# One more transfer from GpSimd, 40 single words from each partition, between attention and routing

## The chip, the cores and the metric

The kernel runs on one core of a Trainium2 chip. The metric is the device time of one execution in microseconds (us); of several executions the median is given. The core has five engines that run at the same time, each with its own instruction queue: TensorE (PE, with its weight loads as PEld), VectorE (DVE), ScalarE (ACT), GpSimd (POOL) and SyncE (SP). The 16 DMA engines move data between DRAM and the on-chip memory (SBUF). An engine or a queue waits for another only where a semaphore says so.

## What is computed

Two stages, in float32. The first is attention with a block mask: 4 batches, 8 heads, 768 positions, 64 wide, blocks of 32. A query block sees its neighbours, the first and last block, and three blocks drawn for it. The second stage routes the 3072 rows that come out to 8 experts of 384 rows each, greedily by the largest logit, and applies the expert's two matrices:

```python
logits = x @ w_gate                      # x: 3072 x 512, 8 experts
order = np.argsort(-logits.flatten())
for idx in order:                        # largest logit first
    tok, e = int(idx) // E, int(idx) % E
    if assigned[tok] >= 0 or counts[e] >= cap:   # cap = 384
        continue
    assigned[tok] = e; counts[e] += 1
...
h = np.maximum(x[mask] @ w1[e], 0.0)     # for each expert's rows
out[mask] = h @ w2[e]
```

## The kernel before

`tile_kernel` runs `Attn(...).run(start)` and then `Moe(...).run(start)`. Both write out one fixed order of instructions for each engine; the hardware keeps that order within an engine, and semaphores order the engines among each other.

Attention works on pairs of heads and groups of four query blocks. A planner (`Plan`) chooses the order. The rows that it produces go to the DRAM tile `xrows` by SyncE's queue (L628, L638, L640), the logits stay in SBUF as `lg`. GpSimd copies keys and values into place (L276, L370), clears a part of a tile (the memset of L423) and issues gathers of value rows (L401). In the second of the four batches GpSimd also fills the constants of `Start.consts`, among them `places` (L1353): 128 partitions, each holding the numbers 0 to 383 as float32. It is read by `Moe.rows` later and stays in place to the end.

Routing (`Moe.route`, `Moe.search`) finds the expert that fills first and its threshold, by counting how many logits lie above a guess: VectorE counts two thresholds (`jd`) and ScalarE one (`ja`), TensorE sums over the partitions (`pz`), VectorE makes the next guess (`jn`). Two such searches of eight steps stand ahead of the choice of the first expert. Before them `Start.part(1, ...)` prepares the last third of the keys on VectorE (L1383 to L1402). Once the expert is known (`en`, `ei`), GpSimd adds a large negative number to that expert's logits (`lg<-lg,en`), and VectorE takes the next maximum (`c_mx<-lg`). SyncE then loads the first pieces of that expert's weights (`raw`, L1116).

`Moe.rows` turns the threshold into the list of 384 rows, using `places` (`L`) and a running count (`c_M`), and GpSimd gathers those rows from `xrows` in three gathers of 128 (`xg<-xrows,row`). TensorE transposes them and the expert's products begin. From there on the routing of the next experts runs beside the products of the present one. GpSimd then makes the low halves of the weights (`wlo<-raw,whi`), issues the next gathers, and scatters the results (`out_dram<-ot,idx`). Calls in `Moe` that go through the helper `Timed` all bear its line, L816.

All transfers that GpSimd issues are on the queue q0 (software_dynamic), those of SyncE on q1, those of ScalarE on q10.

Of the kernel before, what the change touches and what calls it, by code (L numbers as in the profile page):

```python
# [7 lines left out]
F32 = mybir.dt.float32  # L8
# [1396 lines left out]
def tile_kernel(tc, q, k, v, sampled_blocks, moe_w_gate, moe_w1, moe_w2, out):  # L1405
    nc = tc.nc
    with ExitStack() as ctx:
        ctx.enter_context(tc.manual_schedule())
        cst = ctx.enter_context(tc.tile_pool(name="cst", bufs=1))
        dram = ctx.enter_context(tc.tile_pool(name="dram", bufs=1, space=bass.MemoryType.DRAM))  # L1410
        xd = dram.tile([NT, DM], F32, name="xrows")
        lg = cst.tile([128, NCH, E], F32, name="lg")
        jp = cst.tile([128, 128], I32, name="jp")
        nc.gpsimd.iota(jp, pattern=[[1, 128]], base=0, channel_multiplier=-1)
        ident = cst.tile([128, 128], F32, name="ident")
        nc.vector.tensor_scalar(ident, jp, 0.0, None, op0=OP.is_equal)
        start = Start(nc, cst, lg, jp, ident)
        with ExitStack() as a:
            vs = [dram.tile([S + BS, VR], F32, name=f"vrows{b}") for b in range(B)]
            Attn(a, tc, q, k, v, sampled_blocks, moe_w_gate, xd, vs, lg, ident).run(start)  # L1420
        with ExitStack() as m:
            Moe(m, tc, xd, lg, start.c, moe_w1, moe_w2, out).run(start)


# [27 lines left out]
```

## Time and profile before

| | |
|---|---|
| median of 3 runs | 658.86 us (656.57 to 661.0) |
| profiled execution | 663.22 us, of which the profile's span is 661.4 us |
| mean granted TensorE clock | 0.935 |
| busy, share of the span: TensorE | 563.3 us, 85% |
| VectorE | 423.8 us, 64% |
| GpSimd | 407.2 us, 62% |
| ScalarE | 379.9 us, 57% |
| DRAM traffic | 76.38 MB read, 19.24 MB written |

A share of the span is a mean over stages that differ. What one instruction more is worth is read from the stage in which it stands: attention up to about 302 us, the choice of the first expert up to about 340 us, and the experts from then on. Times in the rows below are us from the start of the span, lengths are us or, where marked, ns.

### The profile page before, as it was taken

The numbers are of one execution on the slowest core, as the hardware profiler recorded it, in microseconds if no ns is written. First come the engines' busy times: TensorE is split into PE (matmuls) and PEld (weight loads), VectorE is DVE, ScalarE is ACT, GpSimd is POOL, SyncE is SP. The second block draws the span as 40 slices with busy tenths as digits, with TensorE's granted clock in tenths as the row PEclk, the third lists the DMA queues.
The fourth block names the chain that finished last, engine by engine and source line by source line (L and its number), as shares of the span: only waits on it lengthen the run. The fifth ranks groups of instructions, "written<-read, shape, count | busy, mean of one in ns | idle before, by whom it ended". The sixth has DMA issues, their size and how long they took to land. (4 is left out here: it accounts for less than half of the span.)

```text
span 661.4 us, 20156 instructions
## 1 busy us (share of the span) xinstructions
PE 563.3 (85%) x7416; PEld 445.7 (67%) x7416; DVE 423.8 (64%) x1630; ACT 379.9 (57%) x846; POOL 407.2 (62%) x741
## 2 busy tenths in 40 slices
PE   5798888789979988863149999999999999999993
PEld 3476656577737765651038788787878878898982
DVE  3677768568756878825776868778786968232110
ACT  4866697558755786624346475565757555445510
POOL 5686757568746876530036485676757677878631
PEclk9898899799989999966568999999999999999997
DMA  9998889887889563300053542626354545445100
GB/s 191 259 229 199 234 223 231 177 225 200 190 183 264 139 172 112 100 18 25 1 164 139 191 161 86 217 82 213 106 192 151 168 144 176 169 166 169 71 16 32
DMA packets 125571, 102.25 MB, mean 155 GB/s; under 512 B 81185, under 2 KB 99745, under 8 KB 125473
## 3 DMA queue, kind: packets, MB, share of 16 engines
q1 hardware_dynamic: 117696, 78.44, 44.0%
q0 software_dynamic: 6912, 22.17, 11.2%
q8 instruction: 58, 0.95, 0.6%
q10 hardware_dynamic: 864, 0.36, 0.2%
q14 instruction: 41, 0.33, 0.2%
HBM read 76.38 MB, written 19.24 MB: 145 GB/s over the span
## 5 line engine op out<-in xcount | busy, mean ns | idle before, releaser
L816 POOL TENSOR_TENSOR wlo<-raw,whi 128x512 fp32r<-128x512 f32 x128 | 161.8, 1291 | 60.6 <-ACT whi L816 60.0
L272 ACT ACTIVATE vw<-vn 32x520 f32<-32x520 f32 (+2 forms) x108 | 68.6, 635 | 29.1 <-PE ps L577 26.7
L276 POOL COPY vw<-vn 32x520 f32<-32x520 f32 (+2 forms) x88 | 54.1, 615 | 46.6 <-DMA vz<-vrows,vidx 22.9
L370 POOL COPY kg<-kT 128x128 f32 x264 | 63.9, 294 | 30.0 <-issue 24.2
L816 PE MATMUL po<-whi,hh 128*128 128x512 f32 x192 | 77.4, 403 | 0.0
L816 PE MATMUL po<-whi,hl 128*128 128x512 f32 x192 | 77.0, 401 | 0.0
L816 PE MATMUL po<-wlo,hh 128*128 128x512 f32 x192 | 76.4, 398 | 0.0
L816 ACT ACTIVATE whi<-raw 128x512 fp32r<-128x512 f32 x128 | 74.2, 621 | 0.2 <-issue 0.2
L482 PE MATMUL ps<-kg,qT 64*32 64x256 f32 x1408 | 57.0, 397 | 14.7 <-POOL kg L370 11.9
L524 DVE TENSOR_REDUCE mn<-ps 128x2 f32<-128x512 f32 x88 | 56.5, 681 | 12.1 <-PE ps L482 11.9
L529 DVE TENSOR_TENSOR s<-ps,mn 128x512 f32<-128x512 f32 x88 | 57.7, 680 | 6.7 <-PE ps L550 6.3
L816 DVE SCALAR_TENSOR_TENSOR hl<-ph,hh 128x384 fp32r<-128x384 f32 x64 | 35.3, 552 | 39.8 <-ACT hh L816 39.8
L816 PE MATMUL ph<-xhi,whi 128*128 128x384 f32 x256 | 59.3, 349 | 0.4 <-ACT xhi L816 0.3
L556 ACT ACTIVATE aT<-ps 128x512 f32<-128x512 f32 x88 | 49.5, 598 | 17.2 <-PE ps L550 10.6
L816 PE MATMUL ph<-xhi,wlo 128*128 128x384 f32 x256 | 58.6, 347 | 0.0
L816 PE MATMUL ph<-xlo,whi 128*128 128x384 f32 x256 | 57.7, 342 | 0.0
L816 ACT ACTIVATE hh<-ph 128x384 fp32r<-128x384 f32 x64 | 31.2, 488 | 45.6 <-PE ph L816 43.8
L550 PE MATMUL ps<-ident,s 128*128 128x128 f32 x352 | 51.4, 287 | 3.5 <-ACT aT L556 1.7
L577 PE MATMUL ps<-vz,aT 128*32 128x65 f32 x1408 | 47.4, 225 | 6.4 <-issue 6.3
L401 POOL DMA_INDIRECT vz<-vrows,vidx x48 | 44.8, 934 | 12.8 <-issue 5.8
L577 PE MATMUL ps<-vw,aT 128*32 128x65 f32 x1408 | 46.6, 227 | 6.0 <-issue 4.9
L482 PEld LDWEIGHTS ps<-kg,qT 64*32 64x32 f32 x1408 | 26.9, 109 | 33.0 <-POOL kg L370 17.3
(226 smaller groups left out, 1246.5 us busy)
## 6 DMA issues: line engine op xcount, KB each, us to landing
raw<-in_moe_w_dram SPq DMA_DIRECT2D x64, 512.0 KB
vz<-vrows SPq DMA_DIRECT2D x120, 65.0 KB
vrows<-vn SPq DMA_DIRECT2D x12, 520.0 KB
st<-in_k_dram SPq DMA_DIRECT2D x24, 256.0 KB
st<-in_q_dram SPq DMA_DIRECT2D x24, 256.0 KB
vn<-in_v_dram SPq DMA_DIRECT2D x24, 256.0 KB
xrows<-xt SPq DMA_DIRECT2D x20, 256.0 KB
vz<-vn SPq DMA_DIRECT2D x12, 260.0 KB
```

The lines of the kernel that those rows point to most:

```text
L272: nc.scalar.activation(o, i, AF.Copy, scale=scale)
L276: nc.gpsimd.tensor_copy(o, i)
L370: nc.gpsimd.tensor_copy(kg()[:, :, g, 128 + 32 * r:160 + 32 * r], kT()[:, :, bass.ds(pv[3 * g + r] * BS, BS)])
L401: nc.gpsimd.indirect_dma_start(out=vz[0:96, g], out_offset=None, in_=self.vs[b], in_offset=bass.IndirectOffsetOnAxis(ap=self.vidx[:, bl[g] ...
L482: nc.tensor.matmul(x["S"][0][32 * g:32 * g + 32, 256 * j:256 * j + 256], qT[h, p, BS * bl[gi]:BS * bl[gi] + BS], kg[h, p, gi], start=True, ...
L524: nc.vector.tensor_reduce(x["mn"][:, 0:2], x["S"][0].rearrange("p (j y) -> p j y", j=2), axis=AX.X, op=OP.min)
L529: nc.vector.tensor_tensor(x["s"].rearrange("p (j t) y -> p j (t y)", j=2), x["S"][0].rearrange("p (j y) -> p j y", j=2), x["mn"][:, 0:2, N ...
L550: nc.tensor.transpose(ps[:, c - c0], x["s"][:, c], self.ident)
L556: nc.scalar.activation(x["aT"][:, c0:c1], x["ps", c0][:, 0:c1 - c0], AF.Exp, scale=-1.0 if w == 4 else 1.0)
L577: nc.tensor.matmul(av[32 * g:32 * g + 32, 2 * j + s], aT[:, 2 * j + t, 32 * g:32 * g + 32], v[:, gi, h], start=t == 0, stop=t == 1)
L816: return f(*args, **kw)
```

## The change

After attention's last instruction and before routing's first, in program order, a DRAM tile of 128 x 40 x 2 words is made, and GpSimd issues a transfer of the first 40 words of each partition of `places` to it. The words lie one behind the other in SBUF; in DRAM every second word is written. 5120 words of 4 bytes are moved, 20 KB. Nothing reads the DRAM tile.

```diff
@@ -1419,6 +1419,8 @@
             vs = [dram.tile([S + BS, VR], F32, name=f"vrows{b}") for b in range(B)]
             Attn(a, tc, q, k, v, sampled_blocks, moe_w_gate, xd, vs, lg, ident).run(start)
         with ExitStack() as m:
+            fill = dram.tile([128, 40, 2], F32, name="fill")
+            nc.gpsimd.dma_start(fill[:, :, 0], start.c["places"][:, 0:40])
             Moe(m, tc, xd, lg, start.c, moe_w1, moe_w2, out).run(start)
```

## Rows read from the trace of the kernel before

**Rows 1.** The page's 40 slices of the span, busy tenths.

```profile
POOL 5686757568746876530036485676757677878631
...
DMA  9998889887889563300053542626354545445100
```

**Rows 2.** Stretches: us, busy us and instructions by engine, clock, DMA share, GB/s.

```profile
core 0: us, PE busy (x) PEld busy (x) DVE busy (x) ACT busy (x) POOL busy (x), PEclk, DMA share, GB/s
...
305.00:310.00 5.00, 0.70 (x5) 0.41 (x5) 3.88 (x24) 1.90 (x7) 0.00 (x0) 0.50 0.00 0
...
315.00:320.00 5.00, 0.66 (x4) 0.32 (x4) 3.81 (x25) 1.65 (x6) 0.00 (x0) 0.50 0.01 3
...
325.00:330.00 5.00, 0.97 (x4) 0.74 (x5) 3.46 (x20) 1.10 (x4) 0.08 (x1) 0.50 0.00 0
```

**Rows 3.** GpSimd's timeline, 280 to 345: start, us, what [idle before <-releaser].

```profile
292.31 0.53 POOL L423 MEMSET vw<- 32x520 f32 x1
329.92 0.59 POOL L816 TENSOR_TENSOR lg<-lg,en 128x192 f32<-128x192 f32 x1 [37.09 <-DVE en L816]
340.30 1.01 POOL L816 DMA_INDIRECT xg<-xrows,row  x1 [9.78 <-DVE pk L816]
...
342.87 0.95 POOL L816 DMA_INDIRECT xg<-xrows,row  x1 [0.30 <-issue]
```

**Rows 4.** Waits of GpSimd, 290 to 345: us in total, times, longest.

```profile
POOL lg L816 <- DVE en L816: 37.1, 1, 37.1
```

**Rows 5.** VectorE's timeline, 329 to 333.

```profile
331.33 0.15 DVE L816 TENSOR_SCALAR ei<-ef 128x1 int32<-128x1 f32 x1
331.40 0.34 DVE L816 TENSOR_REDUCE c_mx<-lg 128x24 f32<-128x192 f32 x1
```

**Rows 6.** GpSimd's groups by form: busy us, mean ns, idle before.

```profile
L401 POOL DMA_INDIRECT vz<-vrows,vidx x48 | 44.8, 934 | 12.8 <-issue 5.8 <-POOL vw L276 1.5 <-DMA vz<-vrows 1.2
...
L816 POOL DMA_INDIRECT out_dram<-ot,idx x24 | 23.7, 989 | 35.0 <-ACT ot L816 32.6 <-issue 1.3 <-ACT ja L816 0.6
L816 POOL DMA_INDIRECT xg<-xrows,row x24 | 23.1, 964 | 16.1 <-DVE pk L816 10.3 <-issue 4.6 <-PE po L816 0.3
```

**Rows 7.** The page's DMA queues: packets, MB, share of 16 engines' span.

```profile
q1 hardware_dynamic: 117696, 78.44, 44.0%
q0 software_dynamic: 6912, 22.17, 11.2%
...
q10 hardware_dynamic: 864, 0.36, 0.2%
```

**Rows 8.** TensorE's timeline, 343 to 350: the transposes of the gathered rows.

```profile
343.80 0.52 PE L816 MATMUL po<-ident,xg 128*128 128x128 f32 x3 [0.28 <-DMA xg<-xrows,row]
...
348.11 0.55 PE L816 MATMUL po<-ident,xg 128*128 128x128 f32 x3 [2.11 <-DMA xg<-xrows,row]
```

**Rows 9.** Scans into c_M (ns min/median/max), and VectorE and GpSimd around the longest.

```profile
L816 DVE TENSOR_TENSOR_SCAN c_M<-c_one,ac x7: 206/209/1285, 333.5 to 557.1; 128x24 bf16<-128x24 f32 x7
...
557.14 1.26 DVE L816 TENSOR_TENSOR_SCAN c_M<-c_one,ac 128x24 bf16<-128x24 f32 x1
...
555.79 2.55 POOL L816 TENSOR_TENSOR wlo<-raw,whi 128x512 fp32r<-128x512 f32 x2 [0.74 <-ACT whi L816]
```

**Rows 10.** VectorE's timeline, 302 to 307: instructions with two inputs in SBUF.

```profile
304.88 0.22 DVE L1390 TENSOR_TENSOR c_eq<-lg,c_mx 128x64 bf16<-128x64 f32 x1
...
305.25 0.22 DVE L1397 TENSOR_TENSOR c_KLi<-c_KLi,c_KHi 128x64 int32<-128x64 int32 x1
```

**Rows 11.** Beside a gather: GpSimd and VectorE near 533, and VectorE's group by form.

```profile
533.13 0.95 POOL L816 DMA_INDIRECT xg<-xrows,row  x1 [0.30 <-issue]
...
533.44 0.14 DVE L816 TENSOR_SCALAR ki<-c_W 128x1 int32<-128x1 f32 x1
...
L816 DVE TENSOR_SCALAR ki<-c_W 128x1 int32<-128x1 f32 x7 | 1.0, 145 | 0.0
```

**Rows 12.** SyncE's queue, 290 to 346: attention's last stores.

```profile
299.69 1.19 SPq L638 DMA_DIRECT2D xrows<-xm  x2
```

## Prediction before the run

> **What bounds the kernel now.** Start with the page's row of 40 slices for GpSimd and for DMA: in the 19th and 20th slice, 45% to 50% of the span, both are at 0 [rows 1]. This is the stretch between attention and the experts, where the first expert is being chosen. The table of stretches says what runs there: VectorE is busy 3.5 to 3.9 of every 5 us, TensorE under 1, GpSimd 0.00 to 0.08, and the DMA share is 0.01 at most [rows 2]. So the end is set here by one serial chain: a threshold search that goes from VectorE to TensorE and back. Nothing on it waits for GpSimd or for a transfer until the choice is made. TensorE's granted clock is 0.50 there, its 1.2 GHz level, because it has only a few small products to do; the change gives it none and takes none.
>
> The timeline of GpSimd then tells exactly when its work is next wanted. Its last attention instruction is the memset at 292.31, which ends at 292.84. The next one is the add on lg at 329.92, after that come three gathers from 340.30 on [rows 3]. The view of waits puts the 37.1 us before the add down to VectorE's en [rows 4]: GpSimd is early, not late. And the add itself has a little room: it ends at 330.51, while the VectorE reduction that reads its result starts at 331.40, right behind ei [rows 5]. GpSimd can thus be 0.89 us late without cost. The room for the new instruction is 331.40 - 0.59 - 292.84 = 37.97 us.
>
> From the gathers on the room is gone: TensorE waits 0.28 and 2.11 us for gathered rows to land [rows 8]; each us by which they come later moves expert 0 and all that follows by about a us.
>
> **The change, part by part.** Nothing is removed or moved. Added are one DRAM tile and one transfer issued by GpSimd. Its source was written by GpSimd itself long before (the iota on places belongs to constants placed during attention), and nobody reads the destination. So the transfer waits for no engine, and no instruction waits for its data. It can cost in three ways only: the time GpSimd spends issuing it, the time the DMA engines spend on it ahead of something that is wanted, and what it takes from VectorE meanwhile.
>
> *Issuing.* The trace of before holds no plain transfer issued by GpSimd, so its price is bounded. The nearest rows are the gathers: 934 ns with 96 rows, 964 ns with 128 [rows 6]. The growth is 30 ns for 32 rows, 0.94 ns a row. The destination keeps every second word, so there are 128 x 40 = 5120 separate pieces. By growth: 0.964 + (5120 - 128) x 0.00094 = 5.7 us. From below: a single instruction that doesn't grow, 0.93 us. From above: the whole 964 ns spread over 128 rows, 7.53 ns a piece, so 38.6 us. I take 5.7 us, because a plain strided piece has no index to be read, and because the only growth shown is the small one; both gathers differ a little in row length, so the slope is rough and I keep the ends. With 0.30 us to issue (the gap ahead of the third gather [rows 3]) it starts near 293.1 and ends near 298.8; by the ends at 294.1 or 331.7. The reader of lg needs GpSimd free by 330.81 (331.40 less the add's 0.59). Cost: 0, 0 and 0.9 us. What hides it is the search on VectorE; without that cover it would cost its whole length, since the add and the gathers are queued right behind it on GpSimd.
>
> *The DMA engines.* The 5120 pieces over 16 engines are 320 for each, taken as evenly shared. The page's queues give a time per packet: q10, the smallest packets (mean 417 B), 0.2% of 16 x 661.4 us over 864 packets, 24 ns; q1 (mean 666 B) 44.0% over 117696, 39.6 ns; q0 (mean 3.2 KB) 11.2% over 6912, 171 ns [rows 7]. For 320 pieces: 7.8, 12.7 or 54.9 us. I take 12.7 us, the middle: these words are nearer to small packets, but q10's share of 0.2% is rounded to one digit, and q1's packets are many and go both ways. From 294 the transfer is then over before 312. Between 305 and 330 the DMA share is 0.01 or less [rows 2], so it is in nobody's way; ahead of that only attention's last stores run, issued up to 300.9 [rows 12], and what they store is first read by the gathers at 340. Cost 0; by the farthest row see rival A.
>
> *VectorE.* Its instructions of the search run beside the gathers later at their usual length. Cost 0; the other end is rival B.
>
> *Tail.* The program's end has one more transfer to be sure of, done 330 us earlier: 0.
>
> **Sum.** 0 + 0 + 0 + 0. Against its own execution: span 661.4 us, run 663.22 us, so 663.2 us after; the bounds of issuing alone make it 663.2 to 664.1. That execution lies 0.7% above the median of the three runs shown, 658.86 us, and a change of nothing leaves the median too: 659.0 us.
>
> **The rivals.** A, *the words drain slowly (slower)*. The gathers go through the same queue q0, the only one of the software kind, so they stand behind the words. It decides from 340.30 + 1.01 - 294.1 = 47 us of drain, 147 ns a word. At q0's 171 ns the drain ends at 349, 7.7 us past the moment when the first gather starts moving, and TensorE's waits for the gathers [rows 8] pass it on whole: 658.9 + 7.7 = 666.6 us. Beyond that each 3.1 ns more a word is 1 us. For it: no row shows single words written to DRAM. Against it: q0's price belongs to packets 800 times larger. The Trainium skill (DMA: Bandwidth & Descriptors, "Queues, rings and completion order") has every engine take one queue's descriptors in order and turn between queues; by that rule the gathers wait behind the words and the weight loads on q1 don't.
>
> B, *VectorE is held while GpSimd issues (slower)*. VectorE's scan into c_M, with two inputs in SBUF, took 1.26 us where its median is 0.209: it ends just behind GpSimd's pair of subtractions (555.79 + 2.55) [rows 9]. The search's preparation has two such instructions, at 304.88 and 305.25 [rows 10]. If the new transfer held VectorE as the subtraction does, they would wait for its end. That decides from 304.88 - 293.1 = 11.8 us of issuing; at 38.6 us the price is 331.7 - 304.88 = 26.8 us, 685.7 us in all; at the 5.7 us that I take it is nothing. Against it: a single-input instruction from SBUF at 533.44, with a gather in progress from 533.13, took 0.14 us, its mean [rows 11]; no view I read has a two-input one beside a gather. The Trainium skill (SBUF — State Buffer, "SBUF: two separate sides") speaks of an exclusive lock on the pair of ports that VectorE and GpSimd share, held for a whole instruction, also against VectorE instructions with two inputs in SBUF if GpSimd's instruction reads SBUF. By the rule, if it counts the transfer, the end is this rival's; by the row at 533.44 it is the sum above.
>
> C, *the words don't go one by one*. In before 48 x 96 + 48 x 128 = 10752 gathered and scattered rows [rows 6] (scatters counted with 128) went in 6912 packets of q0 [rows 7]: fewer packets than rows, so several pieces can share one. Then the drain is shorter still, and the time the same 659 us.
>
> D, *issuing costs more than the gathers' mean*. From 8.6 ns a piece the chain is over 1% late (8.6 x 5120 ns and 0.30 us to issue are 44.3 us, 6.4 us more than the 37.97 of room); at 10 ns it is 51.5 us, 13.5 us late: 672 us. No row speaks for it but the lack of a row.
>
> **How the numbers follow.** Hidden as summed 0.63; C 0.10, same time; A 0.12; B 0.07; D 0.04; and 0.04 for a median that lands lower by the runs' own spread, since no step gains anything. About 1% is what a measurement of this kernel can tell from no change. Within 1%: 0.63 + 0.10 = 0.73; slower by more: 0.12 + 0.07 + 0.04 = 0.23; faster: 0.04. The range starts just under the lowest run before (656.57) and reaches over A's 666.6 to 668; it holds C, the sum and about two thirds of A, some 0.81, and leaves out B, D and a slower drain. The sum's own range is 655.5 to 663.
>
> **What would show it.** GpSimd's timeline: a transfer right behind 292.84, near 6 us long; the idle time before the add on lg down from 37.1 to about 31; the add and the reduction behind it at their old distance from en. If the add starts later than 0.9 us after en, issuing was mis-sized (D). If VectorE's instruction at 304.88 is long or late, B. If the DMA share stays up past 340 and the gathers' landing grows beyond the 2.11 us wait, A. What would make the forecast wrong, above all, is that no row of before writes single words to DRAM: both bounds of the drain come from longer packets.

## The result, and the profile after

The time after is 666.1 us (median of 16 runs, 662.07 to 670.97); beside it on the same chip the kernel before took 662.36 us (16 runs, 656.57 to 665.78). The ratio is 1.0076, with a 95% interval from 1.0052 to 1.0099 (the two medians alone give 1.0056): slower by three quarters of a per cent. (The forecast's 659.0 us rests on the three runs of before shown then; over sixteen before stands at 662.36.) That lies within the 1% of the forecast and within its range, but it is not "no change", and the reasons given for no change do not hold. Two effects of opposite sign lie under it, and the prediction had neither; that they leave so small a sum is luck.

The profiled execution took 664.25 us, its span 662.5. GpSimd first, which is where the prediction looked (start, us, what, idle before):

```profile
290.79 0.53 POOL L423 MEMSET vw<- 32x520 f32 x1
291.27 2.01 POOL L1423 DMA_DIRECT2D fill<-c_places  x1
336.00 0.58 POOL L816 TENSOR_TENSOR lg<-lg,en 128x192 f32<-128x192 f32 x1 [42.72 <-DVE en L816]
346.36 1.03 POOL L816 DMA_INDIRECT xg<-xrows,row  x1 [9.78 <-DVE pk L816]
```

Issuing took 2.01 us and was over at 293.3. GpSimd then waited 42.72 us for VectorE's en, longer than the 37.09 of [rows 3], so GpSimd is even earlier than before. The add on lg and the first gather are 10.4 us apart in both kernels (336.00 to 346.36; 329.92 to 340.30). What came late is VectorE, and it was late already at the first reduction of routing, here in after and then in before:

```profile
310.33 0.21 DVE L1383 TENSOR_REDUCE c_mx<-lg 128x8 f32<-128x64 f32 x1 [11.44 <-issue]
```

```profile
304.27 0.21 DVE L1383 TENSOR_REDUCE c_mx<-lg 128x8 f32<-128x64 f32 x1 [4.61 <-issue]
```

It starts 13.7 us after attention's last value products (L577) end at 296.6; in before it starts at 304.27, 5.6 us after theirs at 298.7. From this reduction to the add the distance is 25.7 us in both. So the search itself, the stretch that the prediction studied, lost nothing; 8.1 us went just ahead of it. ScalarE shows where, in after and, for the copy to lp, in before:

```profile
295.72 0.59 ACT L272 ACTIVATE xT<-ps 128x512 f32<-128x512 f32 x1
303.93 0.28 ACT L272 ACTIVATE lp<-ps 128x128 f32<-128x128 f32 x1 [7.62 <-remote]
304.89 0.18 ACT L272 ACTIVATE lg<-ps 128x8 f32<-128x8 f32 x1 [0.69 <-PE ps L680]
```

```profile
298.97 0.28 ACT L272 ACTIVATE lp<-ps 128x128 f32<-128x128 f32 x1 [0.59 <-PE ps L669]
```

The copy to lp waits for TensorE's product of L669. In before the same copy started at 298.97 after 0.59 us of waiting; here it waited 7.62 us, and the profile puts the end of that wait to no engine's instruction ("remote"). 7.0 of the 8.1 us are this wait. What came late is TensorE's word that the product was done: the trace has the update of its semaphore at 303.91, 7.1 us after the end that the profile puts to the product (296.8; the profile models the ends of products). VectorE was told late too. It waits for the value products ahead of that one, and started 1.4 us behind their end in after, 0.06 us in before:

```profile
296.32 0.30 PE L577 MATMUL ps<-vz,aT 128*32 128x65 f32 x8
297.99 0.17 DVE L605 TENSOR_SCALAR ps<-ps 128x4 f32<-128x4 f32 x1 [3.05 <-PE ps L669]
```

```profile
298.39 0.30 PE L577 MATMUL ps<-vz,aT 128*32 128x65 f32 x8
298.75 0.17 DVE L605 TENSOR_SCALAR ps<-ps 128x4 f32<-128x4 f32 x1 [1.74 <-PE ps L577]
```

The rest of the 8.1 us comes right behind this wait: TensorE had nothing to do from 297 to 304, its granted clock from 304 to 310.3 is 0.50 (1.2 GHz) where before has 0.81 in the same work, and the eight products of L669 for the last rows took 0.92 us instead of 0.69.

What ran in these microseconds is seen in the view of DMA for 286 to 314 (40 slices of 0.7 us; queues with packets, MB, and their share of 16 engines' time). After:

```profile
DMA  0000000451087989990300198284988869667654
GB/s 0 0 0 23 0 0 0 155 220 23 0 6 5 6 6 22 31 9 0 3 0 0 3 15 12 15 26 19 18 31 38 28 41 45 26 29 29 31 48 41
q1 hardware_dynamic: 521, 0.63, 67.2%
q0 software_dynamic: 96, 0.02, 10.6%
```

The same window of the kernel before:

```profile
DMA  0000100000900000180004400000000000000000
q1 hardware_dynamic: 576, 0.66, 7.2%
```

The DMA engines are busy up to 0.9 and, from the 11th slice on, move 48 GB/s at most. The words themselves (q0) take 10.6%. What swells is q1, on which attention's last results are stored: 0.63 MB take 67.2% of the engines' time where 0.66 took 7.2%, and 55 of the 576 packets fall behind this window. By the semaphores in the trace the last of these stores, issued at 299.5, is down at 318.0; in before, issued at 300.3, it is down at 302.3. The words hold up the stores that share the engines with them; below this is called the choke. The program puts no semaphore between the words and these stores, so the remark ahead of the prediction that a queue waits for another only where a semaphore says so does not hold here.

The second effect is at the other end of the kernel. The view of the program's last line shows GpSimd's drain, with minimum, median and maximum in ns, first in before, then in after:

```profile
L1448 POOLq DRAIN  x3: 51/107/9131, 651.5 to 661.2; - x3
```

```profile
L1450 POOLq DRAIN  x3: 46/107/3657, 658.0 to 662.2; - x3
```

Behind the last scatter GpSimd drains for 3.66 us instead of 9.13. The last scatter starts at 651.71 in before and 658.23 in after, the spans end at 661.4 and 662.5: 9.7 us of tail became 4.3, a gain of 5.5.

```profile
651.71 0.97 POOL L816 DMA_INDIRECT out_dram<-ot,idx  x1 [4.38 <-ACT ot L816]
```

```profile
658.23 0.97 POOL L816 DMA_INDIRECT out_dram<-ot,idx  x1 [4.38 <-ACT ot L816]
```

In this execution that makes +8.1 ahead of routing and -5.5 at the end; attention's own 296.6 against 298.7 us is of the size by which executions differ anyway (295.5 to 302.8 over the kernels below with the same attention).

### The profile page after: what moved, and what is told of

It reads as the page before. It is cut to its first block, busy times and chain, and to the rows that moved or that the text cites. A ratio compares the mean times of both kernels' runs of the same rounds, so it can differ in the third digit from the quotient of the medians.

```text
span 662.5 us, 20158 instructions
## 1 busy us (share of the span) xinstructions
PE 562.8 (85%) x7416; PEld 443.7 (67%) x7416; DVE 424.2 (64%) x1630; ACT 379.7 (57%) x846; POOL 408.7 (62%) x742
## 3 DMA queue, kind: packets, MB, share of 16 engines
q0 software_dynamic: 7008, 22.19, 11.4%
## 5 line engine op out<-in xcount | busy, mean ns | idle before, releaser
L482 PE MATMUL ps<-kg,qT 64*32 64x256 f32 x1408 | 60.2, 410 | 16.8 <-POOL kg L370 10.2
L550 PE MATMUL ps<-ident,s 128*128 128x128 f32 x352 | 49.9, 280 | 3.9 <-ACT aT L556 1.8
L577 PE MATMUL ps<-vw,aT 128*32 128x65 f32 x1408 | 45.4, 223 | 5.1 <-issue 4.5
L577 PE MATMUL ps<-vz,aT 128*32 128x65 f32 x1408 | 45.7, 221 | 2.5 <-issue 2.3
```

Of the source, the lines that this page charges most:

```text
L482: nc.tensor.matmul(x["S"][0][32 * g:32 * g + 32, 256 * j:256 * j + 256], qT[h, p, BS * bl[gi]:BS * bl[gi] + BS], kg[h, p, gi], start=True, ...
L550: nc.tensor.transpose(ps[:, c - c0], x["s"][:, c], self.ident)
L577: nc.tensor.matmul(av[32 * g:32 * g + 32, 2 * j + s], aT[:, 2 * j + t, 32 * g:32 * g + 32], v[:, gi, h], start=t == 0, stop=t == 1)
```

## The experiments

Twelve kernels, each a variant of the changed one, timed beside before in five rounds; the number behind each is the ratio to before with its 95% interval. All do the whole of the reference's work; only the added transfer differs. The theory that the traces suggest: single words written close together in DRAM choke the DMA engines, and attention's end waits for what shares them. Its rivals: any further transfer from GpSimd at this place does it, or the sheer number of pieces does, wherever they go. Lengths named below come from the timelines: the *stage* goes from the end of L577's last products to the reduction into c_mx (5.6 us in before, 13.7 in after), the *drain* is the maximum in the row of the program's end (9.13 and 3.66).

**The same bytes, not in pieces.** The 40 words of a partition are stored side by side, so each partition is one piece.

```
- fill = dram.tile([128, 40, 2], F32, name="fill")
- nc.gpsimd.dma_start(fill[:, :, 0], start.c["places"][:, 0:40])
+ fill = dram.tile([128, 40], F32, name="fill")
+ nc.gpsimd.dma_start(fill, start.c["places"][:, 0:40])
```

> The same 20 KB to DRAM, but as 128 rows of 160 bytes, one behind the other, instead of 5120 single words. Theory W (single words written to DRAM choke the write path; TensorE's completions and attention's last stores stand still behind them): the wait of ScalarE for lp at about 296 us, 7.6 us in the changed kernel, is gone (under 1.5 us), the transfer is done within 4 us, ratio to before 1.000, at most 1.003. Rival G (any transfer that GpSimd issues at this place costs the time, by its issue or its place in q0): ratio 1.007 as with the words.

Measured: 0.9991 (0.9965 to 1.0018), issue 0.62 us, stage 5.6 us, drain 9.21 us. A transfer from GpSimd at this place costs nothing and gains nothing; both effects need the pieces.

**The same pieces into SBUF.** `fill = cst.tile([128, 40, 2], F32, name="fill")` in place of the DRAM tile.

> The same 5120 single words, but to a tile in SBUF, every second word, instead of DRAM. Theory W: no choking, since nothing is written to DRAM: ratio 1.000, at most 1.003, and the wait for lp stays under 1.5 us. Rival D (the 5120 pieces as such keep the DMA engines from everything else, whatever they write to): DMA share high for about 20 us, wait for lp some 7 us, ratio about 1.007.

Measured: 0.9927 (0.9897 to 0.9957), issue 2.04 us, stage 5.6 us, drain 3.66 us. Its row of DMA issues:

```profile
fill<-c_places POOLq DMA_DIRECT2D x1, 20.0 KB, 8.0
```

5,120 single words land in 8.0 us when they go to SBUF, and nothing waits. Cutting into pieces is therefore not what hurts; writing the pieces to DRAM, here 8 B apart, is. That the kernel became *faster* than before was not expected, and led to the drain.

**Twice the words.** `[128, 80, 2]` and `[:, 0:80]`.

> 80 words from each partition instead of 40: 10240 single words to DRAM. Theory W: the drain takes about 40 us instead of some 20 (from 291 to about 331 us), still ahead of the gathers; TensorE's completions stand still for longer, between 7 and 27 us, so ratio between 1.010 and 1.04. A rival by which only the start of the transfer hurts (its issue, or the first packets): ratio 1.007 as with 40 words.

Measured: 1.001 (0.9983 to 1.0036), in neither of the ranges named; issue 3.35 us, drain 3.60 us. The profiled execution took 660.44 us, less than any other of this kernel (median 665.57), so the others lost more than it shows. In it the stage grew by 2.3 us only (ScalarE waited 2.2 us there), but the distance from the add on lg to the first gather grew from 10.4 to 15.3 us:

```profile
329.34 0.58 POOL L816 TENSOR_TENSOR lg<-lg,en 128x192 f32<-128x192 f32 x1 [36.41 <-DVE en L816]
344.67 1.03 POOL L816 DMA_INDIRECT xg<-xrows,row  x1 [14.75 <-issue]
```

Its address list was there in time, as VectorE's search ran at its old pace; the view names no releaser ("issue"), but the trace's semaphores do. Ahead of the gather GpSimd waits from 329.40 to 343.68 for the semaphore of attention's last store into xrows, issued at 297.4, and this one is full at 343.64. So the choke held that store for 46 us, and here the gather paid, as it reads what the store writes: the prediction had these stores as first wanted at 340, and in this run they were not down by then. Twice the words do not cost twice; where the cost falls moves with them.

**The same words, 256 B apart.** `fill = dram.tile([128, 40, 64], F32, name="fill")`; everything else as in after.

> The same 5120 single words to DRAM, 256 bytes from each other instead of 8. Theory W1 (each short write to DRAM is dear by itself): drain about 20 us and ratio about 1.007 as before. Theory W2 (neighbouring words in one short stretch of DRAM wait for one another): drain under 8 us, wait for lp under 2 us, ratio at most 1.003.

Measured: 0.9884 (0.9841 to 0.9928), 658.2 against 664.31 us (which alone give 0.991), issue 2.01 us, stage 5.6 us, drain 3.65 us. The order of instructions is after's on every engine; only the distance of the words in DRAM differs, and it moves the time from 0.76% slower to 1.2% faster. Landing:

```profile
fill<-c_places POOLq DMA_DIRECT2D x1, 20.0 KB, 11.3
```

That is W2, neighbouring words wait for one another, though the landing is above the 8 us that W2 was given.

**Rows far apart, words 8 B apart.** `fill = dram.tile([128, 1280, 2], ...)`, written at `fill[:, 0:40, 0]`, so that the rows of two partitions lie 10 KB apart.

> The 5,120 words land 8 B apart within each partition's row, as in the changed kernel, but the rows of the 128 partitions lie 10 KB apart in DRAM, as in the run with words 256 B apart. Theory N1 (what chokes is each row's own words lying side by side): choked as in the changed kernel, last attention product to the first routing reduction 10 to 14 us instead of 5.6, tail from the last scatter 4.25 us, ratio 1.003 to 1.010. Theory N2 (what chokes is the rows of different partitions, written by different DMA engines, lying 320 B apart): no choke, that stage 5.6 us, tail 4.25 us, ratio 0.987 to 0.993.

Measured: 1.0026 (0.9993 to 1.0059), stage 10.5 us, drain 3.66 us. In the DMA view for 286 to 330 q1 takes 47.5%, and 8.1% in the kernel with 36 words 256 B apart. It is the neighbours within a row that choke (N1). The ratio is smaller than after's; if the rows' distance helps a little, or if this is spread between executions, isn't settled.

**Words 64 B apart.** `[128, 40, 16]`.

> Words 64 B apart in DRAM, issued where the changed kernel issues them: between the 8 B that choke (landing 24.2 us when alone, attention to routing 13.7 us) and the 256 B that do not (landing 11.3 us, 5.6 us). If only words that lie closer than 64 B hurt one another: landing about 11 us, stage 5.6 us, ratio 0.987 to 0.993. If neighbours at 64 B still do: landing over 16 us, stage over 7 us, ratio 0.995 to 1.005.

Measured: 0.992 (0.9886 to 0.9954), stage 6.5 us, drain 3.65 us; q1 takes 27.4% of the engines' time from 286 to 314, between 15.7% at 256 B and 67.2% at 8 B. The landing has no row. Neighbours at 64 B still slow what runs beside them, but the stage has room for nearly all of it: the answer lies between the two that were named. The 0.9 us by which it is longer are again a wait for TensorE (ScalarE's xT for L651, 1.30 us; 0.36 in before).

**The choke at another time.** The words 8 B apart, taken from kh0, which VectorE writes just before the search, and issued behind that write:

```
+ nc.gpsimd.dma_start(self.fill[:, :, 0], c["kh0"][:, 152:192])   # in Moe.run, behind start.part(1, self.pz)
```

> The changed kernel's 5,120 words, 8 B apart in DRAM, but taken from the tile kh0 that VectorE finishes at 306.1 us before the routing search, and issued behind it: about 6 us after attention's last store has landed instead of 9 us before its last product. Theory C1 (the choke costs only through what runs beside it at the end of attention, its stores and TensorE's last products): attention to routing 5.6 us, search 25.7 us, first gather 10.4 us behind the add on lg, tail 4.25 us, ratio 0.987 to 0.993. Theory C2 (it holds back whatever engine is on the path, wherever it falls): 5 to 10 us longer in the search or ahead of the first gather, ratio 1.000 to 1.008.

Measured: 0.9901 (0.9864 to 0.9939), stage 5.6, search 25.7, to the first gather 10.4 us, drain 3.65 us. Issued at 305.49, the words have the DMA engines nearly to themselves (queues and issues, 306 to 330):

```profile
q0 software_dynamic: 96, 0.02, 11.6%
q14 instruction: 2, 0.02, 2.0%
...
fill<-c_kh POOLq DMA_DIRECT2D x1, 20.0 KB, 24.2
```

Set beside the spread words: 24.2 us from issue to landing for neighbours alone on the engines, 11.3 us for words 256 B apart that had attention's stores beside them. The backlog is there all the same, but it falls into the search, where no engine on the path wants a transfer (C1). The cost of the change is thus one of time and place: in after the words were issued at 291.27, 5 us before the end of the last value products and 8 us ahead of attention's last store (298.92).

**The choke among weight loads.** The same transfer issued in the expert stage, behind a set of scatters.

```
+ if k == 2:
+     nc.gpsimd.dma_start(self.fill[:, :, 0], c["kh0"][:, 152:192])   # ahead of self.ffn(k)
```

> The words 8 B apart, from the tile kh0, issued in the expert stage behind expert 0's three scatters (about 393 us), where TensorE is busy 19.8 of 20 us, weights are being read all the time, and no result is stored for 36 us. Theory T (the choke stops TensorE's completions by itself, as it seemed to at attention's end): TensorE idle for 5 us or more between 393 and 420 us, ratio 0.998 to 1.006. Theory C (it holds writes that are under way beside it, and reads of DRAM and TensorE go on): TensorE's busy time in 20 us stays 19.5 or more, first gather to end 315 to 318 us as with the other 40-word transfers, ratio 0.987 to 0.993. A rival between them (reads of weights are slowed): DMA share up, weight conversions waiting for loads, ratio 0.993 to 1.000.

Measured: 1.0044 (1.0014 to 1.0073), stage 5.6 us, drain 3.66 us. The transfer was issued at 432.25, one expert later than the expectation had placed it; the windows to read are those from there on. DMA from 428 to 470, 40 slices of 1.05 us, in this kernel and then in before:

```profile
GB/s 0 0 250 246 172 90 3 6 5 5 0 0 0 16 0 3 18 9 5 22 45 14 29 59 55 28 53 40 89 222 364 367 370 368 382 388 402 357 244 310
```

```profile
GB/s 0 0 0 98 152 258 246 4 0 0 0 0 16 0 0 16 288 361 314 137 311 378 397 274 68 281 180 0 78 207 211 176 127 240 217 195 277 53 0 0
```

Where before reads weights at up to 397 GB/s, this one gets 3 to 59 GB/s until about 457, some 25 us behind the issue. TensorE loses time (columns: stretch, its length, busy us of PE, PEld, DVE, ACT, POOL, granted clock, DMA share, GB/s):

```profile
450.00:460.00 10.00, 6.57 (x28) 4.62 (x28) 5.88 (x33) 3.22 (x10) 2.51 (x2) 0.83 0.57 81
460.00:470.00 10.00, 7.44 (x35) 5.15 (x35) 4.58 (x29) 4.73 (x15) 7.94 (x7) 1.00 1.02 354
```

TensorE, busy 9.93 and 10.00 us in these two stretches of before, loses 5.9 us; the third and fourth expert's first gathers are 45.1 us apart (416.83 and 461.97) instead of 37.9 (418.53 and 456.41). Most of it are two waits for ScalarE's ja, and they have different causes:

```profile
446.54 0.60 PE L816 MATMUL ph<-xlo,whi 128*128 128x384 f32 x2
450.64 0.49 ACT L816 ACTIVATE hh<-ph 128x384 fp32r<-128x384 f32 x1 [3.09 <-PE po L816]
452.13 0.17 PE L816 MATMUL pz<-c_cnt,c_G 128*128 128x5 bf16 x1 [2.10 <-ACT ja L816]
459.84 1.15 ACT L816 ACTIVATE whi<-raw 128x512 fp32r<-128x512 f32 x2 [3.94 <-DMA raw<-in_moe_w_dram]
461.48 0.17 PE L816 MATMUL pz<-c_cnt,c_G 128*128 128x5 bf16 x1 [2.59 <-ACT ja L816]
```

The second is a load of weights: ScalarE's conversion, and ja behind it, waited 3.94 us for one. That is the rival in the middle, at a higher price than it was given: reads on q1 are held too. The first is theory T. ScalarE's hh reads a product that ended at 447.14 and started 3.5 us later; the trace has no update of TensorE's semaphore between 446.71 and 450.62, and then five within 0.24 us. VectorE waited for TensorE up to 450.77 as well. So TensorE's completions stood still at the height of the choke here too. Its busy time doesn't show it (9.70 of the 10 us from 440 to 450, as in before), because the profile models the ends of products. The ratio lies in the range that T was given; theory C, by which only writes are held, is out. Instruction packets are slow as well: one on q8 took 4.9% of 14 us on 16 engines, 11 us (440 to 454), against 0.4%, 0.9 us, in before (438 to 452):

```profile
q8 instruction: 1, 0.02, 4.9%
```

```profile
q8 instruction: 1, 0.02, 0.4%
```

**Fewer words.** 28 and 36 words of each partition, 256 B apart.

> 28 words of each partition instead of 40 (3,584 instead of 5,120), 256 B apart, so without the choke: the attention-to-routing stage 5.6 us in every theory. It leaves out nothing of the reference's work. Theory L (the gain at the end grows with the words sent): 28/40 of 5.5 = 3.9 us, the last scatter to the end 5.9 us instead of 9.7, ratio 0.994. Theory S (all or nothing: the end is short once GpSimd's transfers of the run have passed some count of pieces): 9.7 us and ratio 1.000 if this is below the count, 4.25 us and 0.990 if above.

Measured: 0.9979 (0.9948 to 1.0011), stage 5.6 us; the drain is long:

```profile
L1450 POOLq DRAIN  x3: 46/107/9209, 653.2 to 662.9; - x3
```

> 36 words of each partition (4,608), 256 B apart; no choke, stage 5.6 us. Theory L: 36/40 of 5.5 = 5.0 us, last scatter to the end 4.8 us, ratio 0.991. Theory S: 4.25 us and 0.990 if above the count, 9.7 us and 1.000 if below; together with the run of 28 words, two ends of 9.7 and 4.25 us are S, two of 5.9 and 4.8 us are L, and two equal ends leave it open.

Measured: 0.9881 (0.9826 to 0.9936), 655.76 us against 663.39, the stage 5.6 us; the drain is short:

```profile
L1450 POOLq DRAIN  x3: 46/107/3484, 650.4 to 654.4; - x3
```

All or nothing (S): 3,584 words leave the drain as it was, 4,608 shorten it by 5.7 us, and 10,240 (3.60 us) no further. The gain does not grow with the words.

**The words from SyncE's queue.** `nc.sync.dma_start(...)` with the spread tile.

> The words 256 B apart (the transfer that gave 0.9884 from GpSimd), issued from SyncE's queue instead, where it stands behind attention's last stores and ahead of the first weight load of routing. Theory S (the short end comes of GpSimd's own transfers passing a count of pieces): the last scatter to the end 9.7 to 10 us as in the kernel before, ratio 0.997 to 1.003. Rival (any 5,120 pieces shorten the end, whichever queue takes them): 4.25 to 4.5 us, ratio 0.987 to 0.993. Attention to routing 5.6 us in both; SyncE is free until it reads the expert's number at 331 us.

Measured: 0.9978 (0.9944 to 1.0011), stage 5.6 us, drain 9.13 us: no gain, so the short drain belongs to GpSimd's own transfers. SyncE issued it in 0.60 us, and its queue shows how differently it cuts (window 286 to 330, where the kernel with GpSimd's spread words has 576 packets on q1):

```profile
q1 hardware_dynamic: 5712, 0.68, 12.1%
```

5,136 packets more for 5,120 words, one each; GpSimd's q0 has 96 more packets for the same words.

**The words at 79 us.** The spread transfer from GpSimd, right behind the iota on places.

> The words 256 B apart, from GpSimd, but issued at 79 us, right behind the iota that writes the constant, with the whole of attention to come. Theory S (only the run's count matters, not the place): last scatter to the end 4.2 to 4.5 us, ratio 0.987 to 0.995 with at most 2 us of GpSimd lost in attention. Rival (the short end needs the transfer late, behind GpSimd's attention work): 9.7 to 10 us, ratio 1.000 to 1.003. In both the attention-to-routing stage is 5.6 us.

Measured: 0.9978 (0.995 to 1.0006), drain 3.66 us, stage 5.6 us. The drain is short wherever the transfer stands (S), but attention ended at 306.5 us, where the other kernels have 295.5 to 302.8: the gain was spent. Two stretches of 20 us, this kernel and then before, same columns as above:

```profile
80.00:100.00 20.00, 14.77 (x276) 11.92 (x276) 9.05 (x26) 12.78 (x24) 11.95 (x33) 0.74 1.02 171
```

```profile
80.00:100.00 20.00, 17.21 (x379) 12.50 (x378) 14.13 (x38) 19.62 (x39) 11.47 (x24) 1.00 0.87 230
```

The engines, busy all the time in this run (1.02; 0.87 in before), moved 171 instead of 230 GB/s, and TensorE did 276 products instead of 379. So spread words are likely not free either: they need a stretch in which the engines have nothing better to do. One trace doesn't show it, as TensorE was 2.0 us behind before's busy time already in the 20 us ahead of the transfer; but the median gained nothing either.

## Why the prediction was wrong, point by point

**Issuing** (taken 5.7 us, 0.93 to 38.6): 2.01 us, hidden as said. With 0.62 us for 128 pieces, 1.61 for 3,584, 2.01 for 5,120 and 3.35 for 10,240 a piece costs 0.26 to 0.29 ns, where the slope between two gathers gave 0.94. The room of 37.97 us was never touched; GpSimd's idle time grew, as en came later. Rival D (8.6 ns a piece; the 6.4 us it named are 0.97% of 659, not over 1%) falls with it.

**The DMA engines** (12.7 us, cost 0): the step that failed. Its first half was a price: 7.8 to 54.9 us by the mean packets of three queues, 12.7 taken. Issued late and alone the words took 24.2 us to land, inside the bounds and nearly twice the value taken; for words 256 B apart (11.3) or in SBUF (8.0) the value would have been fair. The second half was the error that cost: "it is in nobody's way". The sentence itself named what was in the way, attention's last stores, and wrote them off because their data is first read at 340. Two things were missed. Those stores do not run at their own pace beside the words: some 0.6 MB went from 7.2% to 67.2% of the engines' time, and the last of them landed 18.5 us after its issue instead of 2.0. And the work ahead of routing was not safe either: TensorE's last product for lp reached ScalarE 7.0 us late. The Trainium skill (DMA: Bandwidth & Descriptors, "Back-pressure in remote DMA") says, of writes to another core, that stalled writes stall the other queues of their engine too; here the writes are local, and the traces show another queue held all the same, on stores (after) and on loads (e12_mid's 3 to 59 GB/s).

**Rival A** (words drain slowly, the gathers behind them on q0) had the cause, a slow drain, and the wrong victim. It was to decide from 47 us of drain; 24 us was enough, since the first to wait was not the gather on q0 but what was already running on q1. That its 666.6 us stand so near to the 666.1 measured is luck: in after the first gather follows the add by 10.4 us, as in before. By the rule that A cited from the Trainium skill (DMA: Bandwidth & Descriptors, "Queues, rings and completion order"), engines turn between queues, and weight loads on q1 wouldn't wait; the weight loads in the run among the experts (e12_mid) waited, with 3 to 59 GB/s instead of up to 397.

**Rival B** (VectorE held while GpSimd issues): nothing. L1390, one of the two instructions it named, took 0.23 us after (0.22 in [rows 10]), and issuing was long over. No run had a VectorE instruction with two inputs in SBUF beside the issuing, so whether it would be held is not shown.

**Rival C** (several words share a packet) is what happened: q0 grew from 6912 [rows 7] to 7008 packets.

```profile
q0 software_dynamic: 7008, 22.19, 11.4%
```

Its conclusion, a shorter drain of words and so the same time, does not follow: 96 packets carried the words, and in e8_late they occupied the engines for 11.6% of 24 us, 2.8 us, while the words took 24.2 us to land. Packets are not what the time is made of here, and a price per packet, from whichever queue, could not have given it.

**Tail** ("one more transfer to be sure of, done 330 us earlier: 0"): the second term that failed, with the other sign. GpSimd's drain, which no row of the prediction shows, is 9.13 us in before and 3.66 in after. "No step gains anything" was wrong by 5.5 us of the path. Had only the choke been there, the change would have been slower by over 1%: kernels with the short drain and no choke, or hardly any, stand at 0.988 to 0.993 (e10_early apart, which lost its gain elsewhere), so by the ratios the choke takes 1.0076 - 0.990 = 1.8%, some 12 us. The profiled execution shows 8.1; whether other executions lose more at the same place can't be read from one trace.

**What the prediction would have needed.** It argued from what waits for the new transfer's data and from averages of packets. The question that decides was what else is moving on the same engines in the 20 us behind it, and who waits for that; and its own remark that no row of before writes single words to DRAM was the right warning, given too little weight against a range of prices that all belonged to rows of other kinds.

**What stays open.** Why TensorE's completions come late while the engines are choked: 1.4 and 7.1 us in after, 3.5 us in e12_mid, and no transfer is listed between product and reader. In e8_late, with the same words but one small product of the search about every 1.2 us and no other transfer under way, none was late; which of the two made the difference isn't tested, nor whether the slow instruction packets or the writing of the profile's own records have a part in it. Removing the choke (e4_spread), or moving it behind attention (e8_late), removes the wait. Why GpSimd's drain is short above some count between 3,584 and 4,608 words isn't shown either; only that it is a step, that it belongs to GpSimd's queue, that whole rows don't bring it about (e1_rows), and that place, target and spacing don't matter to it.

## What to carry to other kernels

A transfer that nobody waits for can still set the time, through the transfers that share its engines: look at what is under way in the 20 us behind its issue, and who reads that next. Single words written side by side to DRAM are the worst case of this (24.2 us for 20 KB); the same words 256 B apart, in SBUF, as whole rows, or issued into a stretch without transfers cost nothing at this place. At 79 us, among attention's transfers, even the words 256 B apart brought no gain. And read the program's last line as well: 9 us of a 660 us kernel stood in GpSimd's final drain, and the two best kernels of this study, 0.988 of before, owe their gain to that row, as far as the traces show: it gives 5.5 to 5.7 of the 6 to 8 us, and the rest lies within the intervals.

## What the runs showed of the hardware

- Words 8 B apart in DRAM landed in 24.2 us for 5,120; 256 B apart in 11.3 us; in SBUF in 8.0 us. At 64 B the stores beside them took 27.4% of the engines' time, against 67.2% at 8 B and 15.7% at 256 B.
- While words 8 B apart land, transfers of q1 are held: weight loads got 3 to 59 GB/s instead of up to 397 (e12_mid), and attention's last store took 18.5 us instead of 2.0 (after), 46 us with twice the words (e3_double). Instruction packets are slow too: one took 11 us instead of 0.9 (e12_mid).
- Beside such words and other traffic TensorE's completions came up to 7.1 us late (after) and 3.5 us late (e12_mid), while the profile counts TensorE as busy or idle as if they had not.
- GpSimd packs words, 5,120 into 96 packets, and issues them in 2.01 us; SyncE sends 5,136 packets for the same words and issues in 0.60 us.
- GpSimd's drain at the program's end took 9.1 to 9.2 us in every kernel with at most 3,584 added single words from GpSimd (none, whole rows, or words from SyncE among them) and 3.5 to 3.7 us in every kernel with at least 4,608.
